# Four small edits to the hand-ordered start of a retention and mixer kernel: state products by head, a transpose in another pool, two copies shared out by tile, one block moved

## The chip, the cores and the metric

The kernel runs on one core of a Trainium2 chip. The time is the device time of one execution in microseconds (us). Before the change the median of three runs is 329.42 us (328.65 to 330.31). One more execution was recorded by the hardware profiler; it took 328.29 us, and its span, from the first to the last instruction, is 326.3 us. Engines are named as the profile names them: PE multiplies matrices, PEld is its load of stationary operands, DVE, ACT and POOL work elementwise, SP issues DMA transfers. A queue of POOL issues transfers too.

## The reference

There are 8 batches, 8 heads, 576 positions and a head dimension of 64, so a row of the model has 512 numbers.

```python
scores = scale * q @ k^T                        # per batch and head
ret    = scores * gamma[h] ** (i - j) for i >= j, else 0
x      = ret @ v                                # heads side by side: (8, 576, 512)
u      = x + ((x^T @ U) @ V)^T                  # U: 576x32, V: 32x576, mixes positions
out    = u + relu(u @ w_ch1) @ w_ch2            # 512 -> 2048 -> 512
```

## The kernel before, in words

**Retention in chunks.** The decay is split into a factor for the query's position (`qscale`) and one for the key's (`vscale`), so each batch can be worked through in chunks of positions. Within a chunk the scores are masked and multiplied with v. What came before the chunk enters through a state, the sum over earlier positions of k times scaled v. The state of a head is 64x64. Two heads lie together in one 128x128 block, of which only the two diagonal 64x64 quarters mean anything.

**Batches 0 and 1 go first, in units.** The first two batches are done by hand-ordered code (`startup`, `first_stretch`): four units u = 0 to 3 of 256 positions each (two of batch 0, two of batch 1) and one odd chunk J of 128 rows, whose lower half (LO) ends batch 0 and whose upper half (HI) begins batch 1. For a unit, `load_u` fetches q, k and v (SP), `cast_unit` makes bf16 of k and then q (POOL, L600), `scale_u` scales v (POOL, L604), `T_u` transposes k (j = 1) and q (j = 0) with 8 transposes each on PE (L615) into a tile `pst`, which DVE (L628) or ACT (L626) copies out. `SC_u` forms scores (L643) for half the heads, `mask_u` masks them (DVE, L651), `RV_u` multiplies with v (L669), `QS_u` adds the earlier state (L678), and `XS_u` scales the result into x (DVE, L686).

**State products.** `ST_u` (L692) accumulates the state of a unit: for four pairs of heads and two interleaved halves jj, one product of 128x128 outputs (L695), whose off-diagonal quarters nobody reads. Its rows argument is LO or HI (64 rows of contraction) or ALL (128). `Sblk` (L708) copies the two diagonal quarters into `sblk` (L704 on ACT, or L706 on DVE). `ST_J` (L774, product L778) does the same for a half of chunk J. In `startup` three accumulators are begun by unit 0 (`accA`, `accB`, `accC`) and unit 1 adds to two of them. In `first_stretch` one accumulator `acc` is begun by `ST_J(HI)` and units 2 and 3 add to it.

**Pools of accumulators.** A tile of a pool can be reused only when its last reader is done. `ps_sc` (tag psc), `ps_o` (po) and `ps_s` (pss) hold one tile each, `ps_big` (big) three in rotation. `ps_s` serves in turn the chunk J result `poJ`, the small product `pu_o` of `make_uo` (L178), and the state sums. `ps_big` serves transposes, Y1 and the three first tiles of `xT`.

**The mixer.** `x` of a batch is transposed into `xT` (L873, L973), `MA` forms the rank-32 product (L414), its expansion is added in the same accumulator (L888, L987), and the sum is copied as `uT` into bf16 by ACT and DVE. The four column groups cc of batch 1's `xT` are halves of two tiles: cc = 0 and 1 of one `ps_sc` tile, cc = 2 and 3 of one `ps_o` tile. The copies (L992) alternate between ACT and DVE by cc % 2. `MH` (L441) forms `u` itself.

**The two large products.** Y1 (L500) multiplies a 128-wide block f (of 16) of `w_ch1` with `uT`: four products of 128x512 per block, and a relu on ACT (L505). Y2 (L534) multiplies with `w_ch2`. In `first_stretch` the function `y(n)` drops the next n Y1 blocks of batch 0 at chosen places between the steps of units 2 and 3; the engines work strictly in the order of the code. I write f0 to f15 for these blocks. The weights of four blocks come in one transfer, `load_w1(fb)` (L202, on POOL's queue): the one for f8 to f11 is issued inside unit 2, behind that unit's casts, and the one for f12 to f15 inside unit 3.

**After that** each later batch's retention is spread as filler through the large products of the batch before it (`merge`, `spread`). There SP carries the input loads, the transposes of q and k by DMA (`xbar`, L269) and of u (L458).

Order of PE around the change, before: `ST_u(1)` twice, `RV_u(1)`, `xT`, `MA`, expansion, `T_J(HI)`, f0, `make_uo`, `SC_J`, f1, `ST_J`, f2; unit 2: `T_u` (k, q), f3, f4, `SC_u`, f5, `ST_u(LO)`, `SC_u`, f6, `ST_u(HI)`, `RV_u`, `QS_u` twice, f7, `RV_u`; unit 3: `T_u`, f8, f9, `SC_u`, f10, `ST_u(LO)`, `SC_u`, f11, `RV_u`, `QS_u` twice, `RV_J`, f12, `RV_u`; `xT`, f13, `xT`, `MA1`, `xT`, f14, expansion, the four `uT` copies with f15 beside them, then batch 1's Y1.

Of the kernel before, what the change touches and what calls it, by code (L numbers as in the profile page):

```python
# [10 lines left out]
BF16 = mybir.dt.bfloat16  # L11
# [31 lines left out]
def kernel(  # L43
# [11 lines left out]
    nc = tc.nc  # L55
# [546 lines left out]
    def scale_u(u, hh, eng):  # L602
        o, f = unit_views(u, 2, hh)
        eng.tensor_tensor(  # L604
            out=o, in0=f,
            in1=vscaleU[:, u, :, 4 * hh:4 * hh + 4].rearrange("p j h -> p h j")[
                :, :, :, None].to_broadcast([P, 4, 2, D]),
            op=ALU.mult,
        )

    def T_u(u, j, eng):
        pst = ps_big.tile([P, 2 * NHP, P], BF16, tag="big", name="pst")
        for jj in range(2):
            for hp in range(NHP):
                nc.tensor.transpose(  # L615
                    pst[:, jj * NHP + hp, :], un[u][j][:, jj, hp * P:(hp + 1) * P], ident)
        t = qkT_pool.tile([P, 2 * NHP, P], BF16, tag="qkT", name="qkT")
        un[u]["T", j] = t
        o, i_ = t, pst
        if j == 0:  # L620

            o = t.rearrange("p a b -> p (a b)").rearrange(
                "p (hp t j) -> p j hp t", hp=NHP, j=2)
            i_ = pst.rearrange("p (j hp) t -> p j hp t", j=2)
        if eng is nc.scalar:
            nc.scalar.activation(out=o, in_=i_, func=AF.Copy)  # L626
        else:
            eng.tensor_copy(out=o, in_=i_)  # L628
# [60 lines left out]
            in1=qscale[:, i0:i0 + n, :, None].to_broadcast([P, n, H, D]), op=ALU.mult,  # L689
        )  # L690

    def ST_u(u, rows, acc, start):  # L692
        for hp in range(NHP):
            for jj in range(2):
                nc.tensor.matmul(  # L695
                    acc[:, hp, :], un[u][1][rows, jj, hp * P:(hp + 1) * P],
                    un[u][2][rows, jj, hp * P:(hp + 1) * P],
                    start=(start and hp == 0 and jj == 0), stop=True,
                    skip_group_check=True,
                )  # L700

    def copy(eng, out, in_):
        if eng is nc.scalar:
            nc.scalar.activation(out=out, in_=in_, func=AF.Copy)  # L704
        else:
            eng.tensor_copy(out=out, in_=in_)  # L706
# [6 lines left out]

    LO, HI, ALL = slice(0, HALF), slice(HALF, P), slice(0, P)

    def T_J(r):
        c = ch[0, J]
        pst = ps_big.tile([P, 2 * NHP, P], BF16, tag="big", name="pst")
        for j in range(2):
            for hp in range(NHP):  # L720
                nc.tensor.transpose(
                    pst[:, j * NHP + hp, r], c["qk"][r, j, hp * P:(hp + 1) * P],
                    ident[r, r])
        if "qkT" not in c:
            c["qkT"] = qkT_pool.tile([P, 2 * NHP, P], BF16, tag="qkT", name="qkT")
        nc.scalar.activation(out=c["qkT"][:, :, r], in_=pst[:, :, r], func=AF.Copy)
# [47 lines left out]
    def ST_J(r, acc):  # L774
        c = ch[0, J]
        vf = c["v"].rearrange("p h d -> p (h d)")
        for hp in range(NHP):
            nc.tensor.matmul(  # L778
                acc[:, hp, :], c["qk"][r, 1, hp * P:(hp + 1) * P],
                vf[r, hp * P:(hp + 1) * P],  # L780
                start=(hp == 0), stop=True, skip_group_check=True,
            )

    def pss_tile():
        return ps_s.tile([P, NHP, P], FP32, tag="pss", name="pss")
# [6 lines left out]
    def startup():  # L792
        load_u(0, (1, 0))
        load_v_rows()
        load_u(1, (1, 0))
        load_u_rows()
        load(0, J, (1, 0), seg=0)
        load_u(0, (2,))
        load_u(1, (2,))
        load(0, J, (2,), seg=0)  # L800
        load(0, J, (1, 0, 2), seg=1)
        load_u(2, (1, 0, 2))
        load_u(3, (1, 0, 2))
        nc.gpsimd.memset(st["x", 0][HI, J, :], 0.0)

        warm(10)
        cast_unit(0)
        T_u(0, 1, nc.vector)
        warm(5)
        T_u(0, 0, nc.scalar)  # L810
        warm(4)
        SC_u(0, 0, ps_sc, "psc")
        mask_u(0, 0)
        cast_unit(1)
        T_u(1, 1, nc.scalar)
        SC_u(0, 1, ps_o, "po")
        mask_u(0, 1)
        warm(2)
        T_u(1, 0, nc.scalar)
        cast_qk(0, J, LO, nc.gpsimd)  # L820
        scale_u(0, 0, nc.gpsimd)
        load_w1(0)
        scale_u(1, 0, nc.gpsimd)
        scale_u(1, 1, nc.gpsimd)
        scale_v(0, J, LO, nc.gpsimd)
        load_w1(1)
        cast_qk(0, J, HI, nc.gpsimd)
        scale_v(0, J, HI, nc.gpsimd)
        warm(7)
        T_J(LO)  # L830
        SC_u(1, 0, ps_sc, "psc")
        mask_u(1, 0)
        scale_u(0, 1, nc.vector)
        SC_u(1, 1, ps_o, "po")
        mask_u(1, 1)
        warm(4)
        make_v()
        make_ue()
        SC_J(LO)
        mask_J(LO)  # L840
        warm(1)

        accA = pss_tile()
        accB = ps_big.tile([P, NHP, P], FP32, tag="big", name="pss2")
        accC = ps_big.tile([P, NHP, P], FP32, tag="big", name="pss3")
        ST_u(0, LO, accA, True)
        Sblk(accA, 0)
        ST_u(0, ALL, accB, True)
        Sblk(accB, 1, (nc.scalar, nc.vector))
        ST_u(0, ALL, accC, True)  # L850
        RV_u(0, 0)
        RV_u(0, 1)
        QS_u(0, 1, 0)
        XS_u(0)
        ST_u(1, LO, accC, False)
        Sblk(accC, 2)
        ST_u(1, ALL, accB, False)
        Sblk(accB, 3)
        un[1]["po"] = ps_sc.tile([P, 2, dm], FP32, tag="psc", name="poB")
        RV_u(1, 0)  # L860
        RV_u(1, 1)
        QS_u(1, 0, 1)
        QS_u(1, 1, 2)
        XS_u(1)
        RV_J(LO)
        QS_J(3)
        XS_J(LO)

        xT = [ps_big.tile([P, dm], FP32, tag="big", name="xT") for _ in range(3)]

        def to_xT(i, ccs):
            for cc in ccs:
                nc.tensor.matmul(  # L873
                    xT[cc][:, i * P:(i + 1) * P],
                    st["x", 0][:, i, cc * P:(cc + 1) * P], ident,
                    start=(i == 0), stop=True, skip_group_check=True,
                )

        for i in range(J):
            to_xT(i, range(3))  # L880
        MA, _, _, _ = mixer_items(0, 0, split=True)
        MA((ps_o, "po"))
        xT.append(ps_sc.tile([P, dm], FP32, tag="psc", name="xT"))
        for i in range(J):
            to_xT(i, (3,))
        for cc in range(NCC):
            g = slice(cc * R, (cc + 1) * R)
            nc.tensor.matmul(  # L888
                xT[cc], st["a", 0][g, :], V4[g, HALF:HALF + 4 * P],
                start=False, stop=True, skip_group_check=True,  # L890
            )
        for cc in range(NCC):
            o = st["uT", 0][:, :, cc, :]
            i_ = xT[cc].rearrange("p (s t) -> p s t", t=P)
            if cc % 2 == 0:
                nc.scalar.activation(out=o, in_=i_, func=AF.Copy)
            else:
                nc.vector.tensor_copy(out=o, in_=i_)

    def first_stretch():  # L900
# [3 lines left out]
        def y(n):  # L904
            for _ in range(n):
                fn = next(ys, None)
                if fn is not None:
                    fn()

        _, MH0, _, outs0 = mixer_items(0, 0, split=True)  # L910
        MA1, MH1, MT1, outs1 = mixer_items(0, 1, split=True)
        T_J(HI)
        y(1)
        make_uo()
        SC_J(HI)
# [7 lines left out]
        def unit(u, slots, last):  # L923
            cast_unit(u)
            load_w1(u)
            scale_u(u, 0, nc.gpsimd)
            scale_u(u, 1, nc.gpsimd)
            T_u(u, 1, nc.vector)
            T_u(u, 0, nc.scalar)
            y(2)  # L930
            SC_u(u, 0, ps_sc, "psc")
            mask_u(u, 0)
            y(1)
            ST_u(u, LO, acc, False)
            Sblk(acc, slots[1])
            SC_u(u, 1, ps_sc, "psc")
            mask_u(u, 1)
            y(1)
            if not last:
                ST_u(u, HI, acc, False)  # L940
                Sblk(acc, slots[2])
            else:
                prep(NI)
                load(*order[NI + 2], (1, 0, 2))
            RV_u(u, 0)
            QS_u(u, 0, slots[0])
            QS_u(u, 1, slots[1])
            if last:
                RV_J(HI)
                XS_J(HI)  # L950
            y(1)
            RV_u(u, 1)
            XS_u(u)

# [34 lines left out]
                start=False, stop=True, skip_group_check=True,  # L989
            )  # L990
        for cc in range(NCC):
            copy((nc.scalar, nc.vector)[cc % 2], st["uT", 1][:, 1:5, cc, :],  # L992
                 xT[cc].rearrange("p (s t) -> p s t", t=P))
        y(16)
        Y1, rest = y1_items(1, by_seg=True)
# [80 lines left out]
```

## Time and profile before

| | |
|---|---|
| median of 3 runs | 329.42 us (328.65 to 330.31) |
| profiled execution | 328.29 us, span 326.3 us |
| PE busy | 314.5 us (96% of the span) |
| DVE, ACT, POOL busy | 157.4, 135.7, 80.4 us |
| chain that ended last, by engine | PE 82%, DMA 9%, SP queue 2%, DVE 2%, ACT 1%, issue 2% |
| Y1 (L500) and Y2 (L534) on that chain | 36% and 32% |
| state products L695 on that chain | 1% |

The granted PE clock is full in all 40 slices of the page. The DMA engines are over 90% busy in most slices up to 270 us. A line of a timeline gives start, duration, engine, source line, operation, output and inputs, sizes and a count; what an engine waited for before it stands in brackets. Ends of products are modelled and overlap, so the pace of a group is read from the starts of neighbouring groups.

### The profile page before, as it was taken

The numbers are of one execution on the slowest core, as the hardware profiler recorded it, in microseconds if no ns is written. First come the engines' busy times: TensorE is split into PE (matmuls) and PEld (weight loads), VectorE is DVE, ScalarE is ACT, GpSimd is POOL, SyncE is SP. The second block draws the span as 40 slices with busy tenths as digits, with TensorE's granted clock in tenths as the row PEclk, the third lists the DMA queues.
The fourth block names the chain that finished last, engine by engine and source line by source line (L and its number), as shares of the span: only waits on it lengthen the run. The fifth ranks groups of instructions, "written<-read, shape, count | busy, mean of one in ns | idle before, by whom it ended". The sixth has DMA issues, their size and how long they took to land.

```text
span 326.3 us, 8497 instructions
## 1 busy us (share of the span) xinstructions
PE 314.5 (96%) x3637; PEld 174.4 (53%) x3660; DVE 157.4 (48%) x266; ACT 135.7 (42%) x292; POOL 80.4 (25%) x114
## 2 busy tenths in 40 slices
PE   7899999999999999999999999999999899999996
PEld 3474554655444455467644455467644355467544
DVE  5373554466824375536654375536654465510012
ACT  2547656772200573057700573057700463047400
POOL 6685647021321320131201320131201300110000
PEclk9999999999999999999999999999999999999999
DMA  7999999999997998699995999699985630440012
GB/s 215 231 224 263 231 208 189 190 185 188 243 212 146 259 188 121 117 257 185 199 135 90 279 200 146 128 251 184 195 133 122 170 67 3 115 96 0 2 73 88
DMA packets 151317, 53.26 MB, mean 163 GB/s; under 512 B 131984, under 2 KB 148752, under 8 KB 151280
## 3 DMA queue, kind: packets, MB, share of 16 engines
q1 hardware_dynamic: 144512, 40.40, 72.3%
q0 software_dynamic: 6768, 12.32, 15.7%
q8 instruction: 28, 0.46, 0.7%
q14 instruction: 9, 0.07, 0.1%
HBM read 36.85 MB, written 9.44 MB: 142 GB/s over the span
## 4 chain that ended last, share of the span: by engine, by line
PE 82%; DMA 9%; SPq 2%; issue 2%; DVE 2%; ACT 1%; POOL 0%
PE ps_y L500 36%; PE ps_y L534 32%; DMA uT<-u 4%; DMA qkT<-qk 3%; PE psc L285 2%; PE po L340 2%; DMA stage_t<-in_q_dram 2%; SPq L582 2%; PE pss L695 1%; PE ph L441 1%; PE po L353 1%; PE ps_y L545 1%; PE psc L296 1%; PE pa L414 1%; DVE xt L686 1%
## 5 line engine op out<-in xcount | busy, mean ns | idle before, releaser
L505 ACT ACTIVATE y<-ps_y 128x384 bf16<-128x384 f32 (+2 forms) x192 | 89.5, 489 | 112.8 <-PE ps_y L500 111.7
L500 PE MATMUL ps_y<-uT,w_sb 128*128 128x512 bf16 (+3 forms) x768 | 133.2, 326 | 1.7 <-DMA uT<-u 1.2
L534 PE MATMUL ps_y<-w_sb,y 128*128 128x512 bf16 x537 | 124.1, 379 | 1.7 <-issue 0.8
L500 PEld LDWEIGHTS <-w_sb 128*128 128x128 bf16 x768 | 69.6, 98 | 50.9 <-DMA uT<-u 2.2
L534 PEld LDWEIGHTS <-y 128*128 128x128 bf16 x560 | 52.6, 98 | 61.5
L523 DVE TENSOR_TENSOR o_sb<-ps_y,u 128x512 f32<-128x512 f32 (+2 forms) x38 | 25.2, 662 | 76.3 <-PE ps_y L534 73.9
L526 POOL DMA_DIRECT2D out_dram<-o_sb x31 | 17.2, 554 | 125.2 <-DVE o_sb L523 125.2
L261 POOL TENSOR_TENSOR vt<-stage_t,vscale 128x512 bf16<-128x512 f32 (+1 forms) x29 | 30.5, 1055 | 70.6 <-DMA stage_t<-in_v_dram 53.8
L306 DVE TENSOR_TENSOR ret<-psc,tri 64x512 bf16<-64x512 f32 x54 | 36.9, 684 | 0.4
L322 DVE TENSOR_TENSOR s_f<-psc,s_f 128x256 f32<-128x256 f32 x42 | 17.8, 424 | 35.0 <-PE psc L296 29.9
L447 DVE TENSOR_TENSOR u<-ph,xt 128x1024 bf16<-128x1024 f32 (+3 forms) x24 | 21.8, 950 | 11.0 <-PE ph L441 11.0
L364 DVE TENSOR_TENSOR xt<-po,qscale 128x512 bf16<-128x512 f32 x27 | 18.7, 692 | 7.4 <-PE po L353 6.7
L252 ACT ACTIVATE qk<-stage_t 128x512 bf16<-128x512 f32 x27 | 16.9, 626 | 11.6 <-DMA stage_t<-in_q_dram 11.6
L331 ACT ACTIVATE s_sb<-s_f 128x512 bf16<-128x512 f32 (+1 forms) x27 | 15.6, 576 | 1.8 <-DVE s_f L320 1.5
L420 ACT ACTIVATE a_sb<-pa 128x128 bf16<-128x128 f32 x8 | 2.2, 277 | 31.0 <-PE pa L414 31.0
L651 DVE TENSOR_TENSOR ret<-psc,triU 128x1024 bf16<-128x1024 f32 x8 | 9.7, 1222 | 11.1 <-PE psc L643 11.1
L250 DVE CAST qk<-stage_t 128x512 bf16<-128x512 f32 x27 | 12.4, 466 | 0.1
L600 POOL CAST qk<-stage_t 128x512 bf16<-128x512 f32 x16 | 9.8, 614 | 10.6 <-DMA stage_t<-in_q_dram 7.2
L340 PEld LDWEIGHTS <-ret 128*128 128x128 bf16 x216 | 9.9, 98 | 4.4
L196 PE MATMUL pw<-ident 128*128 128x512 bf16 x33 | 10.2, 450 | 1.4 <-POOL ident masks.py:199 1.4
L340 PE MATMUL po<-vt,ret 128*128 128x64 bf16 x216 | 10.7, 193 | 0.0
L626 ACT ACTIVATE qkT<-pst 128x1024 bf16<-128x1024 bf16 x5 | 6.3, 1259 | 7.6 <-PE pst L615 7.6
(110 smaller groups left out, 169.2 us busy)
## 6 DMA issues: line engine op xcount, KB each, us to landing
stage_t<-in_k_dram SPq DMA_DIRECT2D x32, 256.0 KB, 4.8
stage_t<-in_q_dram SPq DMA_DIRECT2D x32, 256.0 KB, 5.5
stage_t<-in_v_dram SPq DMA_DIRECT2D x32, 256.0 KB, 5.9
out_dram<-o_sb POOLq DMA_DIRECT2D x31, 256.0 KB, 4.0
w_sb<-in_moe_w_ch_dram POOLq DMA_DIRECT2D x4, 512.0 KB, 8.3
w_sb<-in_moe_w_ch_dram POOLq DMA_DIRECT2D x8, 256.0 KB, 8.3
stage_t<-in_k_dram SPq DMA_DIRECT2D x8, 128.0 KB, 4.8
stage_t<-in_q_dram SPq DMA_DIRECT2D x8, 128.0 KB, 4.7
```

What stands on the lines that cost most here:

```text
L252: nc.scalar.activation(out=t[rows, 0, :], in_=c["f", 0][rows].rearrange("p h d -> p (h d)"), func=AF.Copy)
L261: (eng or nc.gpsimd).tensor_tensor(out=c["v"][rows], in0=c["f", 2][rows], in1=vscale[rows, i, :, None].to_broadcast([n, H, D]), op=ALU.mult,)
L306: nc.vector.tensor_tensor(out=ret.rearrange("p (hp hl) i -> p hl hp i", hl=2)[t, :, :, t], in0=c["psc"][t, :, 0:SW].rearrange("p hl (hp i) ...
L322: nc.vector.tensor_tensor(out=f[:, t, :], in0=inc, in1=f[:, 1 - t, :], op=ALU.add)
L340: nc.tensor.matmul(c["po"][:, hl, hp * D:(hp + 1) * D], c["ret"][:, h, :], c["v"][:, h, :], start=(hp == 0), stop=True, skip_group_check=True,
L364: nc.vector.tensor_tensor(out=xt[:, i, :].rearrange("p (hp hl d) -> p hl hp d", hl=2, d=D), in0=c["po"][:, :, 0:NHP * D].rearrange("p hl ( ...
L447: nc.vector.tensor_tensor(out=st["u", par][:, i0 - base:i0 - base + n, w].rearrange("p s (c d) -> p c s d", c=2), in0=ph[k][:, :, 0:n, :], ...
L500: nc.tensor.matmul(ps[:, 0:n, :], w1_sb[:, cc, f * P:(f + 1) * P], st["uT", par][:, c0:c0 + n, cc, :], start=(cc == 0), stop=(cc == NCC - 1),)
L505: nc.scalar.activation(out=st["y1", par][:, f, c0 * P:(c0 + n) * P], in_=ps[:, 0:n, :].rearrange("p s t -> p (s t)"), func=AF.Relu)
L523: nc.vector.tensor_tensor(out=o_sb[:, 0:n], in0=ps[:, 0:n], in1=st["u", par][:, c, w], op=ALU.add)
L526: (nc.sync if last else nc.gpsimd).dma_start(out=out_flat[r0:r0 + P, w], in_=o_sb[:, 0:n])
L534: nc.tensor.matmul(ps, st["y1", par][:, f, c * P:(c + 1) * P], w2_sb[:, f, :], start=(f == 0), stop=(f == NF - 1),)
```

## The change

Four edits, all in the hand-ordered code:

1. `ST_u` gets an argument `wide`. Unit 0's three calls keep the 128x128 products. For units 1, 2 and 3, and for `ST_J`, each product is replaced by two, one per head, of 64x64 outputs on the diagonal quarters.
2. `T_J(HI)` takes its tile from `ps_s` instead of `ps_big`.
3. The four `uT` copies of batch 1 are shared by tile: ACT takes cc = 0 and 1, DVE cc = 2 and 3.
4. In unit 2 one Y1 block is issued ahead of `T_u`, and the one ahead of the second `RV_u` is dropped. Unit 3 keeps its order.

```diff
-    def ST_u(u, rows, acc, start):
+    def ST_u(u, rows, acc, start, wide=False):
+        if wide:
...
         for hp in range(NHP):
             for jj in range(2):
-                nc.tensor.matmul(
-                    acc[:, hp, :], un[u][1][rows, jj, hp * P:(hp + 1) * P],
-                    un[u][2][rows, jj, hp * P:(hp + 1) * P],
+                for hl in range(2):
+                    w = slice(hp * P + hl * D, hp * P + (hl + 1) * D)
+                    nc.tensor.matmul(
+                        acc[hl * HALF:(hl + 1) * HALF, hp, hl * D:(hl + 1) * D],
+                        un[u][1][rows, jj, w], un[u][2][rows, jj, w],
...
-    def T_J(r):
+    def T_J(r, pool_=None, tag="big"):
         c = ch[0, J]
-        pst = ps_big.tile([P, 2 * NHP, P], BF16, tag="big", name="pst")
+        pst = (pool_ or ps_big).tile([P, 2 * NHP, P], BF16, tag=tag, name="pst")
...
     def ST_J(r, acc):
         for hp in range(NHP):
-            nc.tensor.matmul(
-                acc[:, hp, :], c["qk"][r, 1, hp * P:(hp + 1) * P],
-                vf[r, hp * P:(hp + 1) * P],
+            for hl in range(2):
+                w = slice(hp * P + hl * D, hp * P + (hl + 1) * D)
+                nc.tensor.matmul(
+                    acc[hl * HALF:(hl + 1) * HALF, hp, hl * D:(hl + 1) * D],
+                    c["qk"][r, 1, w], vf[r, w],
...
-        ST_u(0, LO, accA, True)
+        ST_u(0, LO, accA, True, True)
...
-        T_J(HI)
+        T_J(HI, ps_s, "pss")
...
             scale_u(u, 1, nc.gpsimd)
+            if not last:
+                y(1)
             T_u(u, 1, nc.vector)
             T_u(u, 0, nc.scalar)
             y(2)
...
             if last:
                 RV_J(HI)
                 XS_J(HI)
-            y(1)
+                y(1)
             RV_u(u, 1)
...
         for cc in range(NCC):
-            copy((nc.scalar, nc.vector)[cc % 2], st["uT", 1][:, 1:5, cc, :],
+            copy((nc.scalar, nc.vector)[cc // 2], st["uT", 1][:, 1:5, cc, :],
                  xT[cc].rearrange("p (s t) -> p s t", t=P))
```

More of the change, by code (lines that the diff above doesn't have):

```diff
@@ L690, in XS_u @@
         )
-    def ST_u(u, rows, acc, start):
+    def ST_u(u, rows, acc, start, wide=False):
+        if wide:
+            for hp in range(NHP):
+                for jj in range(2):
+                    w = slice(hp * P, (hp + 1) * P)
+                    nc.tensor.matmul(
+                        acc[:, hp, :], un[u][1][rows, jj, w], un[u][2][rows, jj, w],
+                        start=(start and hp == 0 and jj == 0), stop=True,
+                        skip_group_check=True,
+                    )
+            return
         for hp in range(NHP):
             for jj in range(2):
-                nc.tensor.matmul(
-                    acc[:, hp, :], un[u][1][rows, jj, hp * P:(hp + 1) * P],
-                    un[u][2][rows, jj, hp * P:(hp + 1) * P],
-                    start=(start and hp == 0 and jj == 0), stop=True,
-                    skip_group_check=True,
-                )
+                for hl in range(2):
[3 more added lines that the diff above has]
+                        un[u][1][rows, jj, w], un[u][2][rows, jj, w],
+                        start=(start and hp == 0 and jj == 0), stop=True,
+                        skip_group_check=True,
+                    )
     def copy(eng, out, in_):
@@ L777, in ST_J @@
         for hp in range(NHP):
-            nc.tensor.matmul(
-                acc[:, hp, :], c["qk"][r, 1, hp * P:(hp + 1) * P],
-                vf[r, hp * P:(hp + 1) * P],
-                start=(hp == 0), stop=True, skip_group_check=True,
-            )
+            for hl in range(2):
+                w = slice(hp * P + hl * D, hp * P + (hl + 1) * D)
+                nc.tensor.matmul(
+                    acc[hl * HALF:(hl + 1) * HALF, hp, hl * D:(hl + 1) * D],
+                    c["qk"][r, 1, w], vf[r, w],
+                    start=(hp == 0), stop=True, skip_group_check=True,
+                )
     def pss_tile():
@@ L845, in startup @@
         accC = ps_big.tile([P, NHP, P], FP32, tag="big", name="pss3")
-        ST_u(0, LO, accA, True)
+        ST_u(0, LO, accA, True, True)
         Sblk(accA, 0)
-        ST_u(0, ALL, accB, True)
+        ST_u(0, ALL, accB, True, True)
         Sblk(accB, 1, (nc.scalar, nc.vector))
-        ST_u(0, ALL, accC, True)
+        ST_u(0, ALL, accC, True, True)
         RV_u(0, 0)
```

## The prediction

> **What bounds the kernel now.** The page comes first: PE is busy 96% of the span at a full granted clock, so the time is PE's own work and the few places where PE waits. I then listed whom PE waited for in the first 62 us, the only stretch that the change touches. In each row: the total wait, how often, the longest one.
>
> ```profile
> PE pst L615 <- POOL qk L600: 1.6, 2, 0.9
> ...
> PE pst L721 <- ACT uT L896: 0.7, 1, 0.7
> ...
> PE ps_y L500 <- DVE uT L706: 0.3, 1, 0.3
> PE xT L873 <- DVE xt L686: 0.2, 1, 0.2
> ```
>
> Seen here: waits are small, and two belong to edits 2 and 3. The wait on L600 lies at 8 and 12.7 us, ahead of the change. Next the chain that ended last (start, us, what), at the edited places:
>
> ```profile
> 20.24 1.10 PE pss L695 x16
> ...
> 25.50 0.59 ACT uT L896
> 26.14 0.39 PE pst L721 x8
> ...
> 34.02 0.55 PE pss L695 x8
> ...
> 50.68 0.60 ACT y L505
> 51.28 0.50 ACT uT L704
> 51.80 0.70 DVE uT L706
> ```
>
> Seen here: every wide set of 8 state products costs 0.55 us on the path, `T_J` stands behind an ACT copy, and the second `uT` copy, on DVE, starts only when ACT's first is done. Last, the timelines of PE and POOL, for what holds the path once PE is earlier:
>
> ```profile
> 30.30 0.81 POOL L202 DMA_DIRECT2D w_sb<-in_moe_w_ch_dram  x1
> ```
> ```profile
> 39.26 2.10 PE L500 MATMUL ps_y<-uT,w_sb 128*128 128x512 bf16 x8
> ```
>
> The first is the issue of the weights of f8 to f11. Its transfer landed 8.6 us after issue, at 38.9; f8 starts at 39.26. **The margin is 0.36 us.** That issue stands on POOL behind casts that wait for input DMA (q of unit 2: casts at 28.94 and 29.74, each after a DMA wait), so no saving on PE makes it earlier.
>
> **The change part by part** (negative is saved).
>
> *Narrow products, price.* 8 wide ones become 16 of 64x64. The nearest rows:
>
> ```profile
> 162.07 0.29 PE L296 MATMUL psc<-vt,qk 64*64 64x64 bf16 x8
> 162.29 0.39 PE L534 MATMUL ps_y<-w_sb,y 128*128 128x512 bf16 x1
> ```
> ```profile
> 22.40 0.44 PE L753 MATMUL poJ<-vt,ret 64*64 64x64 bf16 x8
> 22.76 0.41 PE L761 MATMUL poJ<-sblk,qkT 128*64 128x128 bf16 x4
> ```
>
> The first is the same form: one half of the rows, the two column halves in alternation. From start to start 8 cost 0.22 us, with the change of tile shape to the next group in it. Lower end: L285 beside it, 16 in 0.15 us, uses all four quarters. Upper end: L753 stays in one quarter, 8 in 0.36 us, 45 ns each. The 128-row form (ALL, unit 1) has a column-tiled relative in `MA` (L414): 20 products on four column groups in 0.39 us. I take 0.36 us for 16, twice the row of 8 less a shape change of some 0.08 us (an estimate from those rows), so **-0.19 us a set**; ends 0.15 (-0.40) and 0.72 (+0.17).
>
> [...]
>
> 1. *Unit 1, two sets ahead of `RV_u(1)`*: -0.38. The rest of the chain (`XS_u` on DVE at 22.50, then `xT` at 23.79) hangs on this and moves along; ACT's state copies, 20.82 to 22.40, start earlier too, and `QS_J` at 22.76 stays behind them.
> 2. *`T_J` from another pool.* Today PE waits until 26.14 for an `xT` tile to be copied, spends 0.32 us on `T_J` (26.14 to 26.46), and starts f0. In `ps_s` the previous user, `poJ`, is read by 24.31, so `T_J` runs right after the expansion, below the copies. But f0 needs the last `uT` copy, which ends at 26.82 today, so it ends only some 0.27 earlier. Then the new wait: `make_uo` takes the same single buffer and must wait for ACT's copy of `T_J` (26.57 to 27.17 today, 0.38 earlier by item 1: 26.79), when PE could start at 26.69. `SC_J` needs that copy too, and f1 stands behind both. Net of the two: **-0.14**. If ACT's copy were later by x, all of x would be lost here.
> 3. *`ST_J`*: 4 wide at 0.33 become 8 at 0.22: -0.11. Sum so far -0.63.
> 4. *The Y1 block ahead of unit 2's `T_u`.* Work is moved, not removed: four products, 0.9 us, one relu, no DMA. Without it the -0.63 would be lost: `T_u` starts at 29.92 and its second half needs POOL's cast that ends at 30.35, just when PE arrives today. With f3 ahead, `T_u` starts at 29.92 - 0.63 + 0.93 = 30.22 and its q half at 30.66, after the cast. At the other end, f7 goes from between `QS_u` and `RV_u`; `RV_u` needs the mask that ends at 36.19 today, some 0.8 us before it now would run, so no new wait. Price 0.
> 5. *`ST_u(2, LO)`*: stands between `SC_u` and the next `SC_u`, which takes the one psc tile and waits for the mask: 0.12 until it starts, 1.22 of mask, some 0.04. So `SC_u` to `SC_u` is at least 1.38 us from the end of the first (32.98); today it is 1.52 (to 34.50). **-0.14**, not -0.19.
> 6. *`ST_u(2, HI)`*: -0.19. Sum -0.96 (the q casts of unit 3 end at 37.11, `T_u` would start at 37.4).
> 7. *The gate.* PE would be ready for f8 at 39.26 - 0.96 = 38.30, the weights land at 38.9. f8 starts at about 38.95: **+0.65 given back**, -0.31 remains.
> 8. *f9* starts at 40.34, some 0.2 behind the end of f8, since it needs the `pst` that DVE copies behind `XS_u(2)`. DVE is 0.96 earlier, the gate only 0.65 of that: the 0.2 goes. Sum -0.51.
> 9. *`ST_u(3, LO)`*: as item 5, -0.14. Sum -0.65. f12 comes at 45.74 - 0.65 = 45.09; its weights (issued 37.06, 7.5 us) are there at 44.6: no second gate.
> 10. *`uT` copies.* Today DVE runs from 51.80 to 53.09 because its first copy waits for ACT's read of the same tile. By tile it needs only PE: from about 50.95 to 52.25; ACT's two still end at 52.25 behind the relu of f14. Y1 of batch 1 takes cc in order; its last product starts at 53.14 today and at about 52.75 then. **-0.39**.
>
> Sum **-1.0 us**. What follows is PE's own work until 156 us, with slack of over 1.5 us at most of its inputs: the q and k transposes of batches 2 and 3 land 2 to 3 us ahead of use up to 81 us. So the saving should carry. 328.29 - 1.0 = 327.3 for the profiled execution; that ran 1.1 us below the median, so beside the median shown it is **328.4 us**.
>
> **The rivals.**
>
> 1. *More than the sum.* Later PE waits three times for DMA transposes: 0.43 at 161.8, 0.40 at 235.2, and this:
>
> ```profile
> 255.82 1.90 PE L500 MATMUL ps_y<-uT,w_sb 128*128 128x512 bf16 x8 [1.18 <-DMA uT<-u]
> ```
>
> The transfer behind it took 7.45 us, its sisters at 100 and 207 us 5.1 and 5.2. An engine a microsecond earlier meets other loads in flight, and the wait can go: -1.0 - 1.18 = -2.2, **327.2 us**. If also the gate were gone (the weights land earlier), the ungated sum is -1.5, and with the 1.18 **326.7**. Against it: SP's and DVE's issue orders move with PE, so the phase hardly changes.
> 2. *The edits do nothing on the path*: a gate at f8 in full and the copies held elsewhere leave -0.2, 329.2 us. This lies within the bound and I count it with the forecast.
> [...]
> 4. *Slower: each narrow product pays its own load.* Loads of 64x64 take 102 to 110 ns in L753. At 106 ns a set of 16 is 1.70 us, +1.15: five sets +5.75, `ST_J` +0.5, less 0.53 from items 2 and 10: +5.7, **335 us**. It becomes slower by over 0.5% (1.65 us) from about 60 ns a product (five sets and `ST_J` are 88 products, today 3.08 us in all: 88 x 60 ns = 5.3). Against: even in a single quarter products follow each other at 45 ns.
>
> **How the numbers follow.** 0.5% (1.65 us) is about what a measurement of this kernel can tell from no change. Forecast (rival 2 in it) 0.43, rival 1 0.40, rival 3 0.08, rival 4 0.09. So faster 0.40, same 0.51, slower 0.09. The range, 326.7 to 329.9 us, reaches from rival 1 with the gate gone to rival 3 and leaves out rival 4. The forecast's own range is 327.8 to 329.2.
>
> **What would show it.** Right: sets of L707 at 0.3 to 0.4 us start to start; `T_J` ahead of the end of the first `uT` copy and a wait of 0.1 us of `make_uo` on ACT; a wait of 0.4 to 0.7 us at f8 for the weights; DVE's `uT` copies starting beside ACT's relu, not behind ACT's first copy; PE at the start of batch 1's `MH` (53.45 today) about 1.0 us earlier, and the same difference at 150 us and at the end. Wrong: sets above 0.55 us, a wait at unit 2's `T_u`, no wait at f8, or a difference at 150 us that is gone or doubled at 260.

## The result, and the profile after

The changed kernel is faster: median 326.94 us of 20 runs, against 329.95 us of 20 runs of the kernel before on the same chip. The ratio is 0.9921, 95% interval [0.9895, 0.9946], so 2.6 us less (1.8 to 3.5). The forecast was 1.0 us less. The ratio leaves out executions that ran in the chip's slower state, so it is not quite the ratio of the two medians.

The profiled execution of the changed kernel took 329.42 us, 2.5 us above its own median, and a second one took 329.31. So the gain can't be read from the two profiles' spans. It is read stretch by stretch, against marks that both kernels pass. Its PE waits (in all, times, longest):

```profile
PE psc L285 <- DMA qkT<-qk: 3.7, 4, 1.7
...
PE ps_y L500 <- DMA w_sb<-in_moe_w_ch_dram: 0.5, 1, 0.5
PE ps_y L500 <- ACT uT L910: 0.3, 1, 0.3
PE xT L887 <- DVE xt L686: 0.2, 1, 0.2
```

Against the list of before: the wait of `T_J` and the one on DVE's `uT` copy are gone, f8 waits for its weights, and the waits for the q and k transposes of later batches have grown from 0.8 to 3.7 us. The wait of 1.2 us for `uT` at 255 us is gone too. These are the two rows of before:

```profile
PE ps_y L500 <- DMA uT<-u: 1.2, 1, 1.2
PE psc L285 <- DMA qkT<-qk: 0.8, 2, 0.4
```

PE's timeline in the head, after:

```profile
20.74 0.81 PE L707 MATMUL pss<-qk 64*64 64x64 bf16 x32
21.48 0.64 PE L669 MATMUL poB<-qk,ret 64*128 64x64 bf16 x32
...
25.61 0.40 PE L733 MATMUL pst<-ident,qk 64*128 64x64 bf16 x8
26.35 1.11 PE L500 MATMUL ps_y<-uT,w_sb 128*128 128x512 bf16 x4 [0.34 <-ACT uT L910]
...
39.67 1.90 PE L500 MATMUL ps_y<-uT,w_sb 128*128 128x512 bf16 x8 [0.54 <-DMA w_sb<-in_moe_w_ch_dram]
```

Start to start, two narrow sets take 0.74 us (20.74 to 21.48), where two wide ones took 1.10. `T_J` now stands ahead of the wait for the first `uT` copy, and f8 is held for 0.54 us. DVE's pair of `uT` copies for batch 1, then ACT's:

```profile
51.14 1.29 DVE L718 CAST uT<-xT 128x512 bf16<-128x512 f32 x2 [2.67 <-PE xT L1003]
```
```profile
51.26 1.08 ACT L716 ACTIVATE uT<-xT 128x512 bf16<-128x512 f32 x2
```

DVE's releaser is PE now, and it starts ahead of ACT's first copy instead of behind it.

This execution ran 0.57 us late by 15 us, ahead of all edits, as its first inputs came later (POOL's cast of q starts at 12.57, at 12.01 before, each time behind its DMA). The table gives the later marks as after minus before, less that 0.57.

| start of the mark on PE (us) | before | after | difference less 0.57 | forecast |
|---|---|---|---|---|
| `RV_u(1)` | 21.27 | 21.48 | -0.36 | -0.38 |
| `make_uo` | 27.34 | 27.33 | -0.58 | -0.52 |
| f2 | 29.04 | 28.94 | -0.67 | -0.63 |
| `T_u(3)` | 38.35 | 38.06 | -0.86 | -0.96 |
| f8 | 39.26 | 39.67 | -0.16 | -0.31 |
| first `SC_u(3)` | 41.29 | 41.50 | -0.36 | -0.51 |
| second `SC_u(3)` | 43.16 | 43.24 | -0.49 | -0.65 |
| `MH` of batch 1 | 53.45 | 53.13 | -0.89 | -1.04 |

So in this execution the head did what was forecast, to within 0.16 us at each mark. The difference that was not forecast lies behind it. At 82 and 88 us this execution loses 2.65 us:

```profile
82.40 0.32 PE L285 MATMUL psc<-qkT 64*64 64x64 bf16 x16 [1.73 <-DMA qkT<-qk]
...
88.56 0.32 PE L285 MATMUL psc<-qkT 64*64 64x64 bf16 x16 [0.92 <-DMA qkT<-qk]
```

and between 245 and 258 us it wins 1.35 us, as the wait for `uT` isn't there. The median run probably does better than this one at 80 us. Why the later waits move was the question for the experiments.

### The profile page after: what moved, and what is told of

Its sections match the earlier page's. It is cut to its first block, busy times and chain, and to the rows that moved or that the text cites. A ratio compares the mean times of both kernels' runs of the same rounds, so it can differ in the third digit from the quotient of the medians.

```text
span 327.5 us, 8608 instructions
## 1 busy us (share of the span) xinstructions
PE 315.9 (96%) x3704; PEld 174.4 (53%) x3704; DVE 157.3 (48%) x266; ACT 135.5 (41%) x292; POOL 80.2 (24%) x114
## 4 chain that ended last, share of the span: by engine, by line
PE 79%; DMA 12%; SPq 5%; POOL 1%; DVE 1%; issue 1%; ACT 0%; DVEq 0%
PE ps_y L534 35%; PE ps_y L500 34%; DMA qkT<-qk 5%; DMA stage_t<-in_q_dram 3%; DMA w_sb<-in_moe_w_ch_dram 3%; SPq L582 2%; PE psc L285 2%; DMA stage_t<-in_v_dram 2%; PE po L340 1%; PE ph L441 1%; PE ps_y L545 1%; PE psc L296 1%; PE po L353 1%; SPq L235 1%; SPq L269 1%; PE pa L414 1%
## 5 line engine op out<-in xcount | busy, mean ns | idle before, releaser
L534 PE MATMUL ps_y<-w_sb,y 128*128 128x512 bf16 x560 | 126.2, 379 | 0.0
L285 PE MATMUL psc<-qkT 64*64 64x64 bf16 x432 | 8.6, 198 | 3.7 <-DMA qkT<-qk 3.7
```

Of the source, the lines that this page charges most:

```text
L534: nc.tensor.matmul(ps, st["y1", par][:, f, c * P:(c + 1) * P], w2_sb[:, f, :], start=(f == 0), stop=(f == NF - 1),)
```

## The experiments

The waits behind the head are named by their tiles: `qkT` is the transposed q and k of a chunk, `uT` the transposed `u` of a batch. Three theories stood at first. A: only the work saved in the head counts. B: an earlier arrival at 65 us makes later waits shorter. C: the moved block covers waits that the one profile of before happened not to have. All kernels were timed against the kernel before on the chip of their own set. The median and ratio of each stand in the table below the experiments.

**The changed kernel again**, no edit.

> The changed kernel once more, unaltered, for a second trace. All theories: about 2.6 us below the kernel before (ratio 0.992). What differs is where. Theory A (fixed saving): PE reaches the first SC of batches 2 and 3 (65 us) about 0.9 us earlier than the kernel before does, counted from its own end of warm-up, and the rest of the run takes the same on average; then the true gain is 1.0 us (ratio 0.997) and the 2.6 is the scatter of runs. Theory B (phase): an earlier arrival at 65 us makes later waits for DMA shorter by some 1.6 us on average, so the stretch from 65 us to the end is shorter than in the kernel before. Theory C (cover in the first stretch): in most runs of the kernel before PE waits about 1.5 us more ahead of unit 2's or unit 3's transposes than in its one profile, for casts that wait for input DMA, and the moved block covers that; then there is no such wait here.

Measured: ratio 0.9915, so the gain is real, and A's "the 2.6 is scatter" falls. No wait at unit 2's transposes. The head, though, is another one here. The weights of f8 took 9.63 us to land (8.56 in the first trace of before), and PE waited 1.41 us for them:

```profile
40.56 1.90 PE L500 MATMUL ps_y<-uT,w_sb 128*128 128x512 bf16 x8 [1.41 <-DMA w_sb<-in_moe_w_ch_dram]
```

Two more stops ahead of it are 0.45 us for scaled v (18.07) and 0.41 us with no releaser in the profile (21.14). PE starts `MH` of batch 1 at 54.03, later than before (53.45). So of the two traces of the changed kernel one shows the head's saving and one does not, while the medians of both sets of runs show the gain.

**The kernel before again**, no edit.

> The kernel before once more, unaltered, for a second trace: ratio 1.000. Theory A: PE's landmarks up to 65 us lie as in the first profile (65.0 for the first SC of batch 2) to within 0.6 us, apart from a common shift of the start. Theory B: the same, and later waits for DMA of 2 us or more in all. Theory C: a wait of PE of 0.5 to 1.5 us at unit 2's or unit 3's transposes (L615 after 25 us) on POOL's cast L600.

Measured: ratio 0.9999. The head lies 0.2 us ahead of the first profile throughout, with no wait at unit 2's or 3's transposes: C falls. The wait at 255 us is there again, 1.0 us.

**The changed kernel, late.**

```diff
         for f in range(6):
             Y1(f, 1)
+        warm(4)
         return rest[6:]
```

> The changed kernel with four products of 128x512 into an unread tile at the end of first_stretch (0.9 us of PE work), so that PE arrives at the later stretches as late as before the change. Theory A: -1.0 + 0.9, so -0.1 us against the kernel before (ratio 1.000). Theory B: the arrival is that of before, so the later waits are too: 0 us, ratio 1.000. Theory C: -2.6 + 0.9 = -1.7 us, ratio 0.995.

Measured: ratio 0.9984 [0.9952, 1.0016]. It fits A and B, hardly C. By itself it decided little: its profile is free of the wait at 255 us, which by B it should have kept.

**The kernel before, early.** Four Y1 blocks leave out the last quarter of their sum.

```diff
-            for cc in range(NCC):
+            ncc = NCC - 1 if by_seg and seg == 0 and 2 <= f < 6 else NCC
+            for cc in range(ncc):
```

> The kernel before, leaving out the last quarter of the contraction in four Y1 blocks of batch 1 (four products of 128x512, 0.9 us of PE work, at 54 to 58 us), with none of the four edits. Theory A: -0.9 us, ratio 0.997. Theory B: -2.5 us, ratio 0.992, as the arrival alone decides. Theory C: -0.9 us, ratio 0.997.

Measured: ratio 0.9994 [0.9958, 1.0031]: 0.9 us less work in the head, and nothing gained. The profile doesn't test B, though: this execution met POOL's casts at unit 2's transposes (0.47 us up to 30.86), and PE reaches the first `SC` of batch 2 at 65.03 us, as before (65.04). It does show PE waiting 4.0 us for `qkT`, where before waited 0.8. So less work in the head isn't passed on by itself, which speaks against A, and the waits for `qkT` vary by more than the whole gain.

One thing that differs between the six traces is a DMA queue of the page that the prediction didn't use, first before, then after:

```profile
q8 instruction: 28, 0.46, 0.7%
```
```profile
q8 instruction: 29, 0.48, 0.6%
```

These are 28 and 29 packets of 16 KB. They are PE's: from the first to the last of the 28, PE goes through 3410 weight loads and as many products, 253 instructions a packet, and no other engine has as many as 400 in all. Counted as two for each of the 3660 and 3704 loads of the pages, PE has 7320 instructions before and 7408 after, 28.9 and 29.3 times 253. In the kernel before, one of them lies inside the `uT` transpose that PE waits for; the window is 248.3 to 255.8 us:

```profile
q8 instruction: 1, 0.02, 1.3%
...
uT<-u SPq DMA_TRANSPOSE x1, 7.5
```

One packet takes 1.3% of 16 engines for 7.5 us, so 1.56 us if a single engine carries it. Theory D: such a block of PE's instructions sits on one of the 16 DMA engines for 1 to 1.5 us; a transpose that is spread over all of them ends when its last part does (one engine for the block and all for the transpose are assumptions, the trace has no row for each engine); and the 88 instructions that the change adds shift every later block against the work.

**The same number of instructions, none of the edits.** Warm-up products are cut into narrower ones, where PE waits for input.

```diff
-            nc.tensor.matmul(
-                ps, ident, ident[:, None, :].to_broadcast([P, 4, P]), start=True, stop=True)
+            for c in cuts:        # [1, 1, 1, 1] for the first 14, [2, 1, 1] for one, else [4]
+                nc.tensor.matmul(
+                    ps[:, c0:c0 + c, :], ident, ident[:, None, :].to_broadcast([P, c, P]),
+                    start=True, stop=True)
+                c0 += c
```

> The kernel before with 44 more products on PE (88 instructions with their loads), as many as the change adds, but in the warm-up: 15 warm-up products of 512 columns are cut into four or three, with the same columns in all, where PE waits for input anyway. Nothing else is changed. Theory D (fetches of PE's instructions): each 16 KB block of PE's instructions comes by one DMA packet of 1 to 1.5 us on one DMA engine; 88 instructions more move every later fetch earlier against the work, and the one that lies in the uT transpose before 255 us in both traces of the kernel before leaves it: the wait of 1.0 to 1.2 us there goes, head unchanged, so -1.3 us, ratio 0.996, and the block transfer is seen at 245 to 248 us. Theory A (only the work saved in the head counts): ratio 1.000, and the wait of about 1.1 us at 255 us stays.

Measured: ratio 0.9949 [0.9922, 0.9976]. **This alone is some two thirds of the gain, with no edit** (1.7 of 2.6 us, each give or take 0.9), and A falls. (This execution's inputs came early: PE is 1.1 us ahead at unit 1's first set, and 0.6 us at batch 1's `MH`. So it is read in places, and the gain by the medians.) In its profile, 249 to 256 us, there is no block, and the transpose takes 5.5 us:

```profile
q1 hardware_dynamic: 4160, 1.05, 78.0%
q0 software_dynamic: 122, 0.43, 25.3%
issues: line engine op xcount, KB each, median us to landing
...
uT<-u SPq DMA_TRANSPOSE x1, 5.5
```

and PE starts the Y1 products behind it with no wait in brackets:

```profile
254.60 1.89 PE L509 MATMUL ps_y<-uT,w_sb 128*128 128x512 bf16 x8
```

**The change with one whole block more than before.** The same padding of 28 warm-up products.

> The changed kernel with 84 more products in the warm-up in the same way (28 warm-up products cut into four): with the 88 instructions of the change this makes 256 more than before, one whole block, so that the later blocks begin at the same places of the work as in the kernel before. Theory D: the block transfer lies in the uT transpose again and the wait of about 1.1 us at 255 us comes back; only the head's saving is left, -0.9 us against the kernel before, ratio 0.997, 1.3 us slower than the changed kernel. Theory A: as the changed kernel, -2.6 us, ratio 0.992.

Measured: ratio 1.001 [0.9983, 1.0037]: **all of the gain is gone**; D's 0.997 lies just outside the interval. PE is early here, 63.58 us at the first `SC` of batch 2 against 65.04 before, and still the wait for `uT` is back and the waits for `qkT` are long, so **B falls**:

```profile
PE psc L294 <- DMA qkT<-qk: 3.7, 3, 2.4
...
PE ps_y L509 <- DMA uT<-u: 0.6, 1, 0.6
```

**Edit 1 alone**, on the kernel before.

> Edit 1 alone on the kernel before (narrow state products of units 1 to 3 and of chunk J). Work on PE falls by 0.36 us ahead of T_J, 0.1 at ST_J, 0.13 to 0.19 at each later set; but with no Y1 block ahead of unit 2's transposes PE meets the casts of q there: up to 0.4 us of it lost, and the weights of f8 hold it at the old place at 39 us: head -0.3 us at 53 us. Theory D: the instruction count is that of the changed kernel, so the wait at 255 us goes too: -1.6 us, ratio 0.995. Theory A: -0.3 us, ratio 0.999.

Measured: 0.9964 [0.9938, 0.9991]. At `MH` the head is 0.06 us ahead of the first profile (0.3 behind, counted from its own start), so its gain isn't in the head. No wait at 255 us.

**Edits 2, 3 and 4 without edit 1.**

> Edits 2, 3 and 4 without edit 1: the transposes in the other pool, the uT copies by tile, the Y1 block ahead, all state products wide. Head at 53 us: -0.2 to -0.3 from the transposes as far as the weights of f8 let it pass, -0.4 from the copies: -0.6 us. PE's instruction count is that of the kernel before. Theory D: the wait of about 1.1 us at 255 us stays: -0.6 us, ratio 0.998. Theory A: the same -0.6 us if the head's work is all that counts, but then the other 2 us must come from edit 1, and narrow_only shows them in its head.

Measured: 0.9998 [0.9966, 1.003]. The head is only 0.13 us earlier, not 0.6. The wait for `uT` near 255 us is there, but is 0.2 us where D said 1.1 (the transpose took 6.5 us, not 7.5), and `qkT` costs 2.8 us.

The next two complete the square of edits and positions of the blocks.

**Edits 2, 3 and 4 with 88 padding instructions.**

> Edits 2, 3 and 4 (all state products wide), with 44 more products in the warm-up, so that PE has as many instructions as the changed kernel. Theory D (position of the fetches): no wait for uT at 255 us, -1.3 us from that and -0.6 us from the head, ratio 0.994, against 1.000 of edits 2 to 4 without the padding. Theory E (what edit 1 does on PE itself is worth the 2 us, by way of the head): as edits 2 to 4 without the padding, ratio 1.000.

Measured: 0.9931 [0.9905, 0.9957].

**Edit 1 alone with 168.**

> Edit 1 alone, with 84 more products in the warm-up: one whole block of 256 instructions more than the kernel before, so that the blocks begin at the same places of the work as there. Theory D: the wait at 255 us is back, head -0.3 us, ratio 0.999 to 1.002. Theory E: as edit 1 alone without the padding, ratio 0.996.

Measured: 0.9997 [0.9967, 1.0026]; the wait for `uT` is back (1.1 us). So with either set of edits the count of 7408 gives a gain, and 7320 or 7576 none; theory E, that the edits make the difference, falls.

**The weights of f8 in two halves.**

```diff
+        step = W1B // 2 if fb == 2 else W1B
+        for f0 in range(fb * W1B, (fb + 1) * W1B, step):
             nc.gpsimd.dma_start(
-                out=w1_sb[:, :, fb * W1B:(fb + 1) * W1B],
+                out=w1_sb[:, :, f0:f0 + step],
```

> The changed kernel with the weights of f8 to f11 loaded in two transfers of 256 KB, those of f8 and f9 first. It tests the gate of the prediction (PE waits 0.54 and 1.4 us at f8 for these weights in the two traces of the changed kernel). If the whole of the 512 KB has to land: the first half lands about 1 us earlier, the wait at f8 falls below 0.3 us, the head at 53 us is 0.3 to 0.6 us earlier, and the time is 0.4 us below the changed kernel's, ratio to the kernel before 0.990. If the gain of the head is lost again later (waits for qkT at 76 to 88 us grow by as much), the ratio stays at 0.992.

Measured: the wait at f8 is gone, and PE reaches the first `SC` of batch 2 at 63.63 us, earlier than in either trace of the changed kernel. The time is no better: 0.9955 [0.9918, 0.9992]. The 0.990 lies outside the interval. The head's gain passes on at best in part.

**A quarter of a block more.** 32 further products, by the same padding.

> The changed kernel with 32 more products in the warm-up (64 instructions, a quarter of a block). Theory D: blocks come some 4 us earlier against the work than in the changed kernel (about 14 instructions a microsecond there), at about 261 and 243 us, both clear of the uT transpose at 251 to 256: no wait at 255, ratio 0.992 or, if the blocks also move away from the qkT transposes at 70 to 88 us, less. Theory A (only the work in the head counts): 0.992 as well; a ratio above 0.996 would speak against both unless a block is seen inside a transpose that PE waits for.

Measured: 1.0102 [1.0059, 1.0144], **slower than before by 3.4 us and than the change by 6**, with no added work but 32 products cut out of wider ones in the warm-up. The wait at 255 us is absent, as said, but blocks fell into `qkT` transposes that PE waits for. The profiled execution took 336.25 us, 3.4 above the median, so its lines are used for places, not for sizes:

```profile
88.57 0.32 PE L294 MATMUL psc<-qkT 64*64 64x64 bf16 x16 [2.72 <-DMA qkT<-qk]
```
```profile
243.22 0.32 PE L294 MATMUL psc<-qkT 64*64 64x64 bf16 x16 [1.69 <-DMA qkT<-qk]
```

A block began to move at 83.8 and one at 239.9 us, both inside the transpose waited for (issued 80.4, 8.1 us; issued 237.0, 6.2 us). Waits that end at 167, 203 and 278 us have a block 3 to 4 us ahead of them too (165, 199, 274). The expectation considered only the transpose near 250 us. PE also stopped once in the middle of 20 equal products, for 1.01 us, with no releaser in the profile:

```profile
24.80 0.24 PE L423 MATMUL pa<-xt,U_E 128*32 128x128 bf16 x4 [1.01 <-issue]
```

A block had moved from 22.5 to 23.4 us, just ahead of it. PE may have waited for its own instructions here; no row shows it.

All kernels together. "PE instructions" is twice the number of PE's weight loads. "Block" is where the nearest block of PE's instructions began, in us after the issue of the `uT` transpose near 250 us; a dash: the trace has no landing. The three columns on the right are of one execution each. Medians of different sets don't compare, the ratios do: the kernel before had 328.89 us in the set of the first four experiments, 328.53 in that of the next four, 328.72 in that of the last four.

| kernel | PE instructions | median us | ratio to before, interval | block | uT took | wait for uT there | waits for qkT |
|---|---|---|---|---|---|---|---|
| before | 7320 | 329.95 | 1 | +4.8 | 7.5 | 1.2 | 0.8 |
| before_again | 7320 | 329.54 | 0.9999 [0.9972, 1.0025] | +5.1 | 7.3 | 1.0 | 1.3 |
| edits234 | 7320 | 328.87 | 0.9998 [0.9966, 1.003] | +4.5 | 6.5 | 0.2 | 2.8 |
| narrow_pad168 | 7576 | 329.05 | 0.9997 [0.9967, 1.0026] | +5.2 | 7.3 | 1.1 | 2.5 |
| after_pad168 | 7576 | 328.76 | 1.001 [0.9983, 1.0037] | +4.5 | - | 0.6 | 3.7 |
| before_pad88 | 7408 | 326.91 | 0.9949 [0.9922, 0.9976] | -3.7 | 5.5 | 0 | 1.7 |
| narrow_only | 7408 | 326.98 | 0.9964 [0.9938, 0.9991] | -3.5 | 5.6 | 0 | 1.0 |
| edits234_pad88 | 7408 | 326.83 | 0.9931 [0.9905, 0.9957] | -3.5 | - | 0 | 1.1 |
| after | 7408 | 326.94 | 0.9921 [0.9895, 0.9946] | -3.6 | - | 0 | 3.7 |
| after_again | 7408 | 326.5 | 0.9915 [0.9886, 0.9945] | -3.8 | 5.5 | 0 | 2.6 |
| after_half_w1 | 7408 | 328.65 | 0.9955 [0.9918, 0.9992] | -3.7 | 5.2 | 0 | 2.3 |
| after_late | 7416 | 328.27 | 0.9984 [0.9952, 1.0016] | -4.0 | 5.5 | 0 | 1.1 |
| before_early | 7312 | 329.86 | 0.9994 [0.9958, 1.0031] | +8.8 | 5.5 | 0 | 4.0 |
| after_pad64 | 7472 | 332.81 | 1.0102 [1.0059, 1.0144] | -6.2 | 5.4 | 0 | 9.2 |

Read by the block column: where it lies inside the transpose (+4.5 to +5.2), the transpose takes 6.5 to 7.5 us and PE waits 0.2 to 1.2 us, whatever the edits; elsewhere it takes 5.2 to 5.6, and PE doesn't wait. The count sets the place: this block begins with 631 to 634 of PE's loads left to the end in the five traces of 7320 and 7576 instructions, so the 256 between the two counts are one block to within a few instructions, and with 685 or 686 left in the six of 7408. The five with the count of before, or one block more, all stand at 1.000; the four kernels of 7408 without a further edit (five rows) stand at 0.992 to 0.996.

Two rows don't follow from the block near 250 us. `before_early` has it clear of the transpose and no wait there, and gains nothing: its `qkT` waits of 4.0 us take the place. `after_late` has the change's 0.992 and 0.9 us of added work, which gives 0.995, but stands at 0.9984, just beyond.

## Why the prediction came out as it did

**The range held it** (326.7 to 329.9; measured 326.94) and the sign was right, but the likeliest case was not: "within 0.5%" had the larger chance, and the kernel is 0.8% faster. That the range held the time is luck in good part: it reached so far down for rival 1, whose mechanism is not what happened.

- *Narrow products* (0.36 us a set): 0.37 us measured. Pairs that differ in columns alone follow at 23 ns in the trace of the changed kernel, with loads of 102 to 113 ns. Rival 4 falls. The range reached up to 329.9 us for rival 3, a set of 0.72 us at 45 ns a product; no run shows that pace for these products (it is that of L753), and the 23 ns stand in its place.
- *`T_J`*: -0.22 instead of -0.14; the wait of `make_uo` on ACT, 0.1 us in the forecast, doesn't show. *The moved block*: no wait at unit 2's transposes, as said; `before_early`, which lacks it, shows what it is for: there PE waits 0.47 us for the casts.
- *The gate* was right in place. In size it is 0.54 us in the one trace and 1.41 in the other: the weights took 9.03 and 9.63 us to land, not the 8.6 of the sum. *The copies*: -0.40 for -0.39.
- **The step that failed** is the sentence behind the sum, "So the saving should carry", with the list of what each edit adds. It counted products by their time on PE and not as instructions that come by DMA in packets (28 before, 29 after). Two things took its place. The first is the position of PE's instruction blocks: worth -1.7 us (ratio 0.9949, so 0.8 to 2.6 us) with no edit at all. Of this the wait at 255 us is 1.0 to 1.2; where the rest comes from isn't shown. The second is the fate of the head's 0.9 us. With the count of before plus one block nothing of it is left (1.001, though in its trace PE was 1.5 us ahead of before at `MH`). The two other sets of edits in the position of before stand at 0.9998 and 0.9997, but their heads had saved less. In the position of the change some 0.2 to 0.3% may remain (0.9921 and 0.9915 against 0.9949), but the intervals overlap, and edit 1 alone stands at 0.9964. So a gain of the edits' own work is not shown. The prediction's own sign of being wrong appears too: the difference to before in the first trace, with the 0.57 taken off, is -0.88 us at 65 us, +1.95 at 86 and +0.59 at 258.
- *Rival 1* named the wait that went, 1.18 us at 255.82, and gave 327.2 us. Its mechanism, other loads in flight for an earlier PE, is wrong: an earlier PE kept the wait (after_pad168), a PE on time (narrow_only, 64.98 us against 65.04 at the first `SC` of batch 2) lost it.

What stays open: why the saving of the head is lost at 76 to 89 us in some traces. Blocks in those transposes are seen there, but not always: `after_pad168` waits 2.41 us up to 87.6 for a transpose issued at 79.53, and the blocks nearest to it begin at 77.8 and 90.4. Late issue is seen as well: in the first trace of the changed kernel SP is busy 8.92 us with the transpose that it starts at 55.94 (5.91 at 55.88 before), and issues a later one at 77.37 instead of 74.68. No run separates the two. And both profiled executions of the changed kernel had waits at 80 us that its median run can hardly have had; a profile may itself change the odds, which no run tests.

## What to carry to other kernels

Where a kernel leans on DMA transposes just in time, count the instructions that an edit adds on PE, not only their duration: they move later instruction blocks onto or off transfers that PE waits for, worth 0.5% here for 88 idle instructions, and 1.8% between the best and the worst count tried. Before an edit's effect is believed, run it once with as many idle instructions and no edit, and once with the edit and a whole block of padding. And a saving ahead of a stretch that waits for DMA has to be followed to the end; here 0.9 us was saved at 53 us in one trace, and gone at 90.

## What the runs showed of the hardware that was not expected

- PE's instructions arrive by DMA in 16 KB packets on a queue of their own, 28 in the trace of before and 29 in that of after, about 253 instructions each by the count above, and a packet takes 0.89 to 1.69 us before and 0.93 to 1.44 after. What the runs show of the cost falls on other transfers, and so on PE in the end: the `uT` transpose near 250 us takes 6.5 to 7.5 us with such a packet inside and PE waits 0.2 to 1.2 for it, else 5.2 to 5.6 and no wait. No row names a wait of PE for instructions, but two stops of PE with no releaser, 1.01 us at 24.80 (after_pad64) and 0.41 us at 21.14 (after_again), come 0.4 and 1.2 us after such a packet ends and may be one.
- In 14 traces, a transpose of u took a median of 4.3 us to land when no such packet began inside it (65 cases whose landing was traced) and 5.2 us when one did (30); of q and k 4.0 us (112) and 5.8 us (164). Longer transfers are likelier to catch a packet, so part of this is selection; the same transpose near 250 us, 5.2 to 5.6 against 6.5 to 7.5 us, is not.
- Two readers of one accumulator tile on different engines ran one behind the other (DVE's copy at 51.80 was released by ACT's); with the copies shared out by tile they ran together (51.14 and 51.26), 0.4 us sooner. Whether the chip or the program's own ordering held the second one is not shown.
